# Seven-product MLP layers after retention: lo parts moved to VectorE, weights converted in units of 1024 columns, PSUM and row sums laid out anew, one activation instead of two operations

## The chip, the core and the metric

The kernel runs on one core of a Trainium2 chip. TensorE (PE) multiplies matrices out of SBUF into PSUM, VectorE (DVE), ScalarE (ACT) and GpSimd (POOL) compute on tiles of 128 partitions, and SyncE (SP) issues the DMAs. Every engine works through its own queue in order and waits on semaphores for the others. The metric is the device time of one launch in microseconds (us); three runs of the kernel before took 704.94 to 706.64 us, median 705.31.

## The reference

```python
# retention: per head a decaying state, step by step over 768 positions
for t in range(S):
    state = gamma * state + einsum('bhd,bhe->bhde', k[:, :, t], v[:, :, t])
    y[:, :, t] = scale * einsum('bhd,bhde->bhe', q[:, :, t], state)
x = y.transpose(0, 2, 1, 3).reshape(1536, 512)
x = (x @ w_a) * (x @ w_b) @ w_out                  # layer 1: 512 -> 1536 -> 512
h = x @ w_in                                       # layer 2: 512 -> 2048 -> 512
out = (h * (1.0 / (1.0 + exp(-1.702 * h)))) @ w_out2
```

There are 2 sequences of 768 tokens, 8 heads of 64. q, k and v are float32; the five weight matrices arrive as 64-bit floats.

## The kernel before, in words

**Retention.** 12 blocks (2 sequences of 6) of 128 tokens. For block n TensorE computes the scores of block n+1 (`att_scores`, L199), the state's increment (`att_kv`, L227) and the output (`att_av`: from the scores, L245, and from the state, L256). VectorE masks the scores (L208), ScalarE copies the state out of PSUM (L237). POOL scales q and v by decays (`att_q` L174, `att_v` L182) for later blocks. `att_x` copies the output and, on every second block, forms the sums that the next stage wants.

**Exact products from float32r.** TensorE multiplies in the rounded format float32r. So each operand is split: hi is the rounded value (a ScalarE copy with a cast), lo = value - hi (`lo_part`, L65, a TENSOR_TENSOR on POOL or VectorE), and each product is three matmuls: hi x hi, hi x lo, lo x hi.

**Seven products.** The up products (x times `w_a`, `w_b` or `w_in`) are done on 2 x 2 blocks with seven block products instead of eight. The row operands are a11 and a12 (tile `a1`), a22, and four sums (`s12`, `s34`); the weight operands are b11, b21, b22 and four sums made by VectorE (L68, tile `tt`). A `Job` is one pair of 128-column chunks of one up matrix: 12 jobs in layer 1 (six pairs for each of `w_a` and `w_b`), 8 in layer 2. Its seven steps of 12 matmuls (L494, 384 columns) accumulate in three PSUM sets of two banks (x, y, w), with copies and adds between them: ScalarE copies x to y after step 1, keeps `u2` and `u4` after steps 6 and 5, VectorE adds and multiplies into the result `g` (L71, L74), and some multiplies `g<-g,u` go to POOL. In layer 2 `result` runs Sigmoid on ScalarE (L516) and then the multiply. `up_order` interleaves the steps of neighbouring jobs. PSUM is used as two pools of two sets each (`ps_a`, `ps_b`).

**Down products.** `down` multiplies chunks of `g` (split into `ghl`) by the down weights, in blocks of four chunks (FB), for four quarters q of the output: per chunk 3 x 3 matmuls of 512 columns (L673). Two quarters share three PSUM sets. After each block `flush` copies (first block, ScalarE L688) or adds (VectorE L71) PSUM into row sums in SBUF. Six chunks stay in SBUF, the others are spilled to DRAM and loaded again. After layer 1's last block `y_part` makes layer 2's row operands out of the row sums.

**Weights.** A piece is 512 columns of 64-bit words (`wraw`). ScalarE takes the absolute value of the high word (L345) and shifts the low word (L346). VectorE clamps (L351), shifts (L352), sets the sign (L358) and adds the low bits (L364): `wt`. Then come the sums, hi (L377) and lo (L65, on POOL). `w_stream` is a generator; each call of `w_step`, one after each step of the up and down stages, emits the next bit of it. 68 pieces in all.

**What sets the order.** The tile scheduler is off (`tc.manual_schedule`): every engine's queue holds its instructions in the order in which the Python code emits them. So a queue's head that waits holds everything behind it, on VectorE, ScalarE and POOL alike.

Of the kernel before, what the change touches and what calls it, by code (L numbers as in the profile page):

```python
# [15 lines left out]
P = 128  # L16
# [24 lines left out]
def retention_moe_kernel(  # L41
# [25 lines left out]
    def sub(engine, o, a, b):  # L67
        engine.tensor_tensor(out=o, in0=a, in1=b, op=ALU.subtract)  # L68

    def add(engine, o, a, b):  # L70
        engine.tensor_tensor(out=o, in0=a, in1=b, op=ALU.add)  # L71
# [40 lines left out]
    vinv = attp.tile([P, SEQ, H, 1], F32, tag="vinv", name="vinv", bufs=1)  # L112
    gdec = attp.tile([P, SEQ, NP], F32, tag="gdec", name="gdec", bufs=1)
    qdec = attp.tile([P, SEQ, NP, P], F32, tag="qdec", name="qdec", bufs=1)
    zero = attp.tile([P, P], F32, tag="zero", name="zero", bufs=1)

    state = [attp.tile([P, NP, 2, D], F32, tag=f"state{i}", name=f"state{i}", bufs=1) for i in range(2)]
    qv_t, kk_t, q_t, v_t, a_t, x_t = {}, {}, {}, {}, {}, {}
# [52 lines left out]
    def att_q(n):  # L171
        if n < NBLK:
            t = attp.tile([P, NP, P], F32, tag="q", name="q", bufs=3)
            (nc.vector if n == 1 else nc.gpsimd).tensor_tensor(  # L174
                out=t, in0=qv_t[n][:, 0, :].rearrange("p (a t) -> p a t", t=P), in1=qdec[:, n % SEQ], op=ALU.mult
            )
            q_t[n] = t

    def att_v(n):
        if n < NBLK:  # L180
            t = attp.tile([P, H, D], F32, tag="v", name="v", bufs=3)
            nc.gpsimd.tensor_tensor(  # L182
                out=t,
                in0=qv_t[n][:, 1, :].rearrange("p (h d) -> p h d", d=D),
                in1=vdec[:, n % SEQ].to_broadcast([P, H, D]),
                op=ALU.mult,
            )
            v_t[n] = t

    def att_scores(n):  # L190
# [3 lines left out]
        ps = ps_a.tile([P, 2, G], F32, tag="set", name="ps_sc")  # L194
# [21 lines left out]
    def att_kv(n):  # L216
# [3 lines left out]
        if c == 0:  # L220
            kv_t[0] = ps_att.tile([P, NP, D], F32, tag="kv", name="ps_kv")
        ps = kv_t[0]
# [16 lines left out]
    def att_av(n):  # L239
        c = n % SEQ  # L240
        ps = ps_att.tile([P, NP, P], F32, tag="av", name="ps_av", bufs=2)
# [626 lines left out]
```

## Time and profile before

| | us |
|---|---|
| profiled execution, its span | 708.58, 706.8 |
| median of three runs | 705.31 |
| TensorE busy, VectorE, ScalarE, POOL | 608.6, 472.1, 307.4, 330.4 |
| retention (0 to 74 us of the span) | 74 |
| up 1 (74 to 269), 1008 matmuls | 195 |
| down 1 (269 to 384), 432 matmuls | 115 |
| up 2 (384 to 541), 672 matmuls | 157 |
| down 2 (541 to 703), 576 matmuls | 162 |
| tail | 3.8 |

The stages follow one another on TensorE; their bounds are where its matmuls change from one line to the next. A matmul's record lasts longer than the distance to the next one, since matmuls are pipelined, so the pace is read from counts over a stretch. The granted clock of TensorE has two levels in this trace, 1.00 (2.4 GHz) and 0.50 (1.2 GHz). What a stage loses is the time between what its matmuls need at full clock and its length.

### The profile page before, as it was taken

The numbers are of one execution on the slowest core, as the hardware profiler recorded it, in microseconds if no ns is written. First come the engines' busy times: TensorE is split into PE (matmuls) and PEld (weight loads), VectorE is DVE, ScalarE is ACT, GpSimd is POOL, SyncE is SP. The second block draws the span as 40 slices with busy tenths as digits, with TensorE's granted clock in tenths as the row PEclk, the third lists the DMA queues.
The fourth block names the chain that finished last, engine by engine and source line by source line (L and its number), as shares of the span: only waits on it lengthen the run. The fifth ranks groups of instructions, "written<-read, shape, count | busy, mean of one in ns | idle before, by whom it ended". The sixth has DMA issues, their size and how long they took to land. (4 is left out here: it accounts for less than half of the span.)

```text
span 706.8 us, 8931 instructions
## 1 busy us (share of the span) xinstructions
PE 608.6 (86%) x3446; PEld 547.9 (78%) x3446; DVE 472.1 (67%) x541; ACT 307.4 (43%) x479; POOL 330.4 (47%) x279
## 2 busy tenths in 40 slices
PE   9777898999999957899997499999885497899997
PEld 8676798999999956777776489988885375677775
DVE  3658789999898999752448566777889919222222
ACT  4536554654464564361213465566685425111000
POOL 6565246474463546545313335555556708243100
PEclk9978899999999987899999599999998799799999
DMA  9662224442522324513000114445332531212022
GB/s 314 197 213 102 59 90 149 119 154 86 179 60 62 119 89 158 184 46 120 30 1 0 59 51 151 157 182 189 107 117 56 196 108 45 89 48 87 1 77 102
DMA packets 21707, 76.94 MB, mean 109 GB/s; under 512 B 2336, under 2 KB 2464, under 8 KB 21664
## 3 DMA queue, kind: packets, MB, share of 16 engines
q1 hardware_dynamic: 21088, 75.77, 31.8%
q10 hardware_dynamic: 576, 0.59, 0.3%
q8 instruction: 27, 0.44, 0.2%
q14 instruction: 16, 0.13, 0.1%
HBM read 60.62 MB, written 15.73 MB: 108 GB/s over the span
## 5 line engine op out<-in xcount | busy, mean ns | idle before, releaser
L673 PE MATMUL ps<-w,ghl 128*128 128x512 f32 x576 | 138.4, 402 | 23.2 <-DVE sum L71 13.4
L673 PEld LDWEIGHTS ps<-w,ghl 128*128 128x128 f32 x576 | 111.3, 194 | 50.1 <-DVE sum L71 15.9
L65 POOL TENSOR_TENSOR w<-wt,w 128x512 fp32r<-128x512 f32 (+1 forms) x68 | 86.4, 1271 | 99.8 <-ACT w L377 82.1
L673 PE MATMUL ps<-ghl,w 128*128 128x512 f32 x432 | 102.1, 397 | 12.2 <-ACT sum L688 7.1
L71 DVE TENSOR_TENSOR sum<-ps,sum 128x512 f32<-128x512 f32 (+1 forms) x41 | 36.7, 933 | 113.5 <-PE ps L673 105.5
L673 PEld LDWEIGHTS ps<-ghl,w 128*128 128x128 f32 x432 | 82.4, 192 | 31.8 <-ACT sum L688 7.9
L65 POOL TENSOR_TENSOR ghl<-g,ghl 128x1536 fp32r<-128x1536 f32 x22 | 79.3, 3622 | 45.4 <-ACT ghl L579 45.1
L494 PE MATMUL ps<-a1h,w 128*128 128x384 f32 x320 | 79.1, 351 | 15.4 <-ACT ps L531 6.9
L65 POOL TENSOR_TENSOR w<-tt,w 128x512 fp32r<-128x512 f32 x40 | 58.0, 1450 | 69.9 <-ACT w L377 44.2
L494 PE MATMUL ps<-s34h,w 128*128 128x384 f32 x320 | 77.0, 348 | 10.6 <-ACT u L540 6.2
L364 DVE CUSTOM_DVE_ANT_0 wt<-wraw,wt 128x1024 uint16<-128x1024 uint16 x68 | 78.6, 1156 | 6.4 <-DVE wt L358 0.5
L74 POOL TENSOR_TENSOR g<-g,u 128x768 f32<-128x768 f32 x28 | 56.3, 2010 | 56.4 <-ACT g L516 35.6
L377 ACT CAST w<-wt 128x512 fp32r<-128x512 f32 (+1 forms) x68 | 37.7, 555 | 91.1 <-DVE wt L364 62.0
L494 PE MATMUL ps<-s12h,w 128*128 128x384 f32 x320 | 74.9, 336 | 1.8 <-ACT u L537 1.4
L358 DVE SCALAR_TENSOR_TENSOR wt<-wraw,wt 128x512 int32<-128x512 int32 x68 | 73.7, 1084 | 1.4
L494 PEld LDWEIGHTS ps<-a1h,w 128*128 128x128 f32 x320 | 60.4, 199 | 17.6 <-ACT ps L531 7.4
L351 DVE TENSOR_SCALAR wt<-wt 128x512 f32<-128x512 f32 x68 | 55.1, 811 | 24.9 <-ACT wt L345 24.9
L352 DVE TENSOR_SCALAR wt<-wt 128x512 int32<-128x512 int32 x68 | 68.3, 1005 | 2.3
L494 PEld LDWEIGHTS ps<-s34h,w 128*128 128x128 f32 x320 | 58.1, 194 | 15.0 <-ACT u L540 8.9
L579 ACT CAST ghl<-g 128x1536 fp32r<-128x1536 f32 x28 | 40.5, 1473 | 60.7 <-PE ps L673 35.7
L494 PE MATMUL ps<-a,w 128*128 128x384 f32 x240 | 48.2, 352 | 15.7 <-DVE u L71 15.7
L494 PEld LDWEIGHTS ps<-s12h,w 128*128 128x128 f32 x320 | 56.9, 188 | 3.1 <-ACT u L537 2.1
(77 smaller groups left out, 866.8 us busy)
## 6 DMA issues: line engine op xcount, KB each, us to landing
wraw<-in_w_dram SPq DMA_DIRECT2D x68, 512.0 KB, 3.7
spilled<-g SPq DMA_DIRECT2D x16, 768.0 KB, 4.8
g<-spilled SPq DMA_DIRECT2D x16, 768.0 KB, 4.9
qv<-in_att_dram SPq DMA_DIRECT2D x11, 512.0 KB, 6.1
kk<-in_att_dram SPq DMA_DIRECT2D x9, 512.0 KB, 6.8
out_dram<-sum SPq DMA_DIRECT2D x3, 512.0 KB, 2.8
out_dram<-sum SPq DMA_DIRECT2D x6, 256.0 KB, 2.4
kk<-in_att_dram SPq DMA_DIRECT2D x3, 256.0 KB, 5.9
```

Source lines behind the costliest of these rows:

```text
L65: engine.tensor_tensor(out=lo, in0=src, in1=hi.bitcast(F32), op=ALU.subtract)
L71: engine.tensor_tensor(out=o, in0=a, in1=b, op=ALU.add)
L74: engine.tensor_tensor(out=o, in0=a, in1=b, op=ALU.mult)
L351: nc.vector.tensor_scalar(out=t, in0=t, scalar1=F64_LOW, scalar2=F64_HIGH, op0=ALU.max, op1=ALU.min)
L352: nc.vector.tensor_scalar(out=ti, in0=ti, scalar1=3, scalar2=0x3FFFFFFF, op0=ALU.logical_shift_left, op1=ALU.bitwise_and)
L358: nc.vector.scalar_tensor_tensor(out=ti, in0=wraw[i][:, :, 1], scalar=-0x40000000, in1=ti, op0=ALU.bitwise_and, op1=ALU.bitwise_or)
L364: nc.vector.tensor_tensor(out=ti, in0=ti, in1=wraw.pop(i)[:, :, 0], op=ALU.add)
L377: nc.scalar.copy(hi, src)
L494: nc.tensor.matmul(ps[:, b, 0:Q], w_operand(self.key, i, wp)[:, kc * P:(kc + 1) * P], r.operand(i, xp)[:, kc, b * Q:(b + 1) * Q], start=(s ...
L579: nc.scalar.copy(g[:, 0], t)
L673: nc.tensor.matmul(banks[n], l, r, start=(f == block[0] and i == 0), stop=(f == block[-1] and i == 2), skip_group_check=True,)
```

## The change

Names are kept where they can be; line numbers move.

- **Lo parts.** `split` emits the hi copy on ScalarE and notes the lo part; `finish` emits noted lo parts on VectorE one step later. `POOL_LO` is empty, so no weight lo part goes to POOL, and `ghl` and the row operands' lo parts go to VectorE too. POOL keeps q, v and the 12 multiplies `g<-g,u` of layer 1's second matrix.
- **Units.** 34 units of 1024 columns take the place of 68 pieces of 512: a job's four weight blocks in one unit, or two chunks of down weights. Each of the conversion steps is one instruction of 1024 columns (the last reads 2048 half words). The operands lie in `wd` (768 columns: b12.. as loaded) and `wt` (1024: the sums, or two chunks).
- **Retention.** q and v are scaled in halves of 256 columns. Sums and lo parts read and write the output in PSUM (three sets instead of two) and are emitted one or two blocks later; some lo parts of `s34` and a22 wait in the list `later` until the up stage. The first unit is converted in blocks 5 to 12.
- **PSUM.** `ps_x` (two sets of two banks) serves scores, x, w and the down stages' first two groups; `ps_y` (two sets of two banks) the up stages and `ps_d` (four single banks) the down stages. Each quarter has its own sets. In `products` all six matmuls of one half b run before those of the other. The first job of layer 1 works in halves.
- **Row sums between the layers.** Layer 1's last block does the first 1024 columns of all four quarters, then the last 512 of quarters 0, 2, 1, 3. `y_first` splits the first halves on the way; `y_second` computes the sums in place, and their splits are taken from `later` in layer 2's first steps.
- **Layer 2.** Gelu_apprx_sigmoid on ScalarE writes `g` at once; the multiply is gone.

```diff
-    rawp = ctx.enter_context(tc.tile_pool(name="rawp", bufs=3))
-    wa = ctx.enter_context(tc.tile_pool(name="wa", bufs=WA))
-    ps_a = ctx.enter_context(tc.tile_pool(name="ps_a", bufs=2, space=PSUM))
+    rawp = ctx.enter_context(tc.tile_pool(name="rawp", bufs=2))
+    wd = ctx.enter_context(tc.tile_pool(name="wd", bufs=2))
+    up_u = ctx.enter_context(tc.tile_pool(name="up_u", bufs=5))
+    ps_x = ctx.enter_context(tc.tile_pool(name="ps_x", bufs=2, space=PSUM))
...
+            for k in (slice(0, NP),) if n == 1 else (slice(0, 2), slice(2, NP)):
+                mul(nc.vector if n == 1 else nc.gpsimd, t[:, k], q[:, k], qdec[:, n % SEQ, k])
...
+    def split(dst, src, keys=()):
+        hi, lo = dst
+        nc.scalar.copy(hi, src)
+        pend.append((keys, lambda: lo_part(nc.vector, lo, src, hi)))
+    def finish(key=None):
+        for it in [it for it in pend if key is None or key in it[0]]:
+            pend.remove(it)
+            it[1]()
...
-        t = rawp.tile([P, DM, 2], I32, tag="wraw", name="wraw", bufs=3)
+        t = rawp.tile([P, W, 2], I32, tag="wraw", name="wraw", bufs=2)
...
+    def w_lo(kind, key, src):
+        whl[kind, key] = t = w_half.pop((kind, key))
+        n = src.shape[-1]
+        lo_part(nc.gpsimd if key in POOL_LO.get(kind, ()) else nc.vector, t[:, 1, 0:n], src, t[:, 0, 0:n])
...
+    POOL_LO = {}
...
-                for wp, xp in ((0, 0), (0, 1), (1, 0)):
-                    for b in range(2):
+            for b in range(2):
+                for kc in range(2):
+                    for wp, xp in ((0, 0), (0, 1), (1, 0)):
...
             if self.ph == 2:
-                nc.scalar.activation(out=g, in_=src, func=ACTF.Sigmoid, scale=1.702)
-            mul(nc.vector if u is None else nc.gpsimd, g, g, src)
+                nc.scalar.activation(out=g, in_=src, func=ACTF.Gelu_apprx_sigmoid)
+            else:
+                mul(nc.vector if u is None else nc.gpsimd, g, g, src)
...
+        shape = dict(y=2, d=4)[name]
...
+        return pool.tile([P, G] if which == "d" else [P, 2, G], F32, tag="set", name="ps")
...
+            if last and ph == 1:
+                for q in range(4):
+                    a = new_set("x")
+                    for f in block:
+                        product(q, f, (0, 1), [a[:, 0], a[:, 1]])
+                        tick(fb)
+                    flush(q, [(a.rearrange("p c t -> p (c t)"), 0, 2 * G)])
+                    y_first(q, sums)
+                for q in (0, 2, 1, 3):
...
+                    if q >= 2:
+                        y_second(q - 2, sums)
```

POOL's queue in the middle of retention, before (numbers tell tiles of one name apart):

```order
L182 TENSOR_TENSOR v_432<-qv_203,vdec_76 128x512
L65 TENSOR_TENSOR s34l_363<-s_467,s34h_362 128x4x128
L174 TENSOR_TENSOR q_489<-qv_312,qdec_79 128x512
L182 TENSOR_TENSOR v_491<-qv_240,vdec_76 128x512
L174 TENSOR_TENSOR q_539<-qv_384,qdec_79 128x512
L182 TENSOR_TENSOR v_541<-qv_312,vdec_76 128x512
L65 TENSOR_TENSOR s34l_363<-s_566,s34h_362 128x4x128
```

and in the changed kernel:

```order
L75 TENSOR_TENSOR q_429<-qv_243,qdec_81 128x256 x2
L75 TENSOR_TENSOR v_432<-qv_204,vdec_79 128x256 x2
L75 TENSOR_TENSOR q_485<-qv_316,qdec_81 128x256 x2
L75 TENSOR_TENSOR v_488<-qv_243,vdec_79 128x256 x2
L75 TENSOR_TENSOR q_541<-qv_374,qdec_81 128x256 x2
```

The lo part between v and the next q is no longer in this queue; q and v come in halves (x2).

VectorE's queue in the changed kernel where up 1 begins, from the first job's last operand (`wt_913`) to the second job's first (`wd_1007`); before, the lo parts of `s34` and of the weights among them were in POOL's queue:

```order
L66 TENSOR_TENSOR wt_913<-tt_820,wt_913 128x1024
L66 TENSOR_TENSOR s12l_427<-x_870,s12h_426 128x4x128
L66 TENSOR_TENSOR s34l_450<-x_526,s34h_449 128x4x128
L66 TENSOR_TENSOR a22_451<-x_526,a22_451 128x2x128
...
L66 TENSOR_TENSOR s34l_450<-x_845,s34h_449 128x4x128
L409 TENSOR_SCALAR wt_825<-wt_825 128x1024
L410 TENSOR_SCALAR wt_825<-wt_825 128x1024
L416 SCALAR_TENSOR_TENSOR wt_825<-wraw_626,wt_825 128x1024
...
L422 ISA wt_825<-wraw_626,wt_825 128x2048
L69 TENSOR_TENSOR tt_1009<-wt_825 128x256 x2
...
L66 TENSOR_TENSOR wd_1007<-wt_825,wd_1007 128x768
```

Left out are two more pairs of `s34l` and a22, one add into `g` and the other two sums. The lo parts of four earlier blocks now stand ahead of the second job's weights.

VectorE's queue where layer 1 ends, before:

```order
L71 TENSOR_TENSOR sum_2839<-ps_3187,sum_2839 128x1024
L71 TENSOR_TENSOR sum_2839<-ps_3146,sum_2839 128x512
L65 TENSOR_TENSOR a1l_3092<-sum_2839,a1h_3091 128x768
L71 TENSOR_TENSOR s_3267<-sum_2770,sum_2839 128x768
L68 TENSOR_TENSOR s_3267<-s_3267,sum_2770 128x768
L65 TENSOR_TENSOR s12l_3221<-s_3267,s12h_3220 128x2x768
```

and in the changed kernel:

```order
L72 TENSOR_TENSOR sum_2585<-ps_2987,sum_2585 128x512
L66 TENSOR_TENSOR a22_2966<-sum_2585,a22_2966 128x768
L69 TENSOR_TENSOR sum_2490<-sum_2490 128x768
L72 TENSOR_TENSOR sum_2490<-sum_2490,sum_2585 128x768
L69 TENSOR_TENSOR sum_2585<-sum_2585,sum_2490 128x768
L69 TENSOR_TENSOR sum_2585<-sum_2585 128x768
L66 TENSOR_TENSOR s12l_3032<-sum_2531,s12h_3031 128x768
L66 TENSOR_TENSOR wt_3001<-tt_2883,wt_3001 128x1024
L66 TENSOR_TENSOR s12l_3032<-sum_2585,s12h_3031 128x768
```

Before, the lo part of a1 (which layer 2's first step reads) stood behind the last quarter's row sum; now it is split earlier, and what follows the last row sum are the in-place sums and the parts of `s12`.

## Rows read from the trace of the kernel before

**Rows 1.** Busy time by stage: window, five engines, clock, DMA share, GB/s.

```profile
0.00:74.00 74.00, 57.75 (x758) 52.30 (x758) 45.59 (x62) 36.13 (x80) 42.36 (x117) 0.86 0.59 197
74.00:269.00 195.00, 181.62 (x1007) 178.79 (x1008) 175.61 (x212) 105.03 (x172) 99.28 (x67) 0.96 0.33 106
269.00:384.00 115.00, 102.83 (x437) 83.12 (x436) 66.10 (x66) 39.79 (x53) 49.18 (x23) 0.96 0.24 83
384.00:541.00 157.00, 127.50 (x670) 122.19 (x669) 117.66 (x146) 90.83 (x136) 82.11 (x51) 0.91 0.33 115
541.00:703.00 162.00, 138.76 (x580) 111.54 (x578) 66.43 (x57) 35.60 (x42) 57.47 (x22) 0.94 0.25 86
```

**Rows 2.** Two windows of matmuls alone (PE, PEld, clock), and the last matmuls.

```profile
160.00:240.00 80.00, 80.00 (x464) 80.00 (x463) 1.00 0.30 95
...
684.00:696.00 12.00, 12.00 (x55) 9.93 (x54) 1.00 0.20 74
...
697.32 5.78 PE L673 MATMUL ps<-w,ghl 128*128 128x512 f32 x24 [0.78 <-DVE sum L71]
```

**Rows 3.** TensorE's waits: releaser, total us, times, longest.

```profile
PE ps L673 <- DVE sum L71: 18.5, 10, 7.7
PE ps L673 <- ACT sum L688: 17.0, 4, 8.9
PE ps L494 <- DVE u L71: 16.2, 3, 8.3
```

**Rows 4.** Timeline, end of up 1 and in down 2: start, duration, [idle before].

```profile
258.00 4.24 POOL L65 TENSOR_TENSOR ghl<-g,ghl 128x1536 fp32r<-128x1536 f32 x1 [0.65 <-ACT ghl L579]
258.89 3.64 DVE L351 TENSOR_SCALAR wt<-wt 128x512 f32<-128x512 f32 x1
...
264.57 0.95 DVE L71 TENSOR_TENSOR u<-ps,u 128x768 f32<-128x768 f32 x1
...
265.57 4.21 PE L494 MATMUL ps<-a,w 128*128 128x384 f32 x12 [8.33 <-DVE u L71]
...
592.73 7.25 POOL L65 TENSOR_TENSOR ghl<-g,ghl 128x1536 fp32r<-128x1536 f32 x2 [1.03 <-ACT ghl L579]
596.75 3.52 DVE L352 TENSOR_SCALAR wt<-wt 128x512 int32<-128x512 int32 x1
603.61 2.93 PE L673 MATMUL ps<-w,ghl 128*128 128x512 f32 x6 [7.66 <-DVE sum L71]
```

**Rows 5.** Single operations: count, ns shortest/median/longest, first and last start.

```profile
L351 DVE TENSOR_SCALAR wt<-wt x68: 409/419/3721, 58.6 to 593.0; 128x512 f32<-128x512 f32 x68
L352 DVE TENSOR_SCALAR wt<-wt x68: 426/430/3551, 59.1 to 596.7; 128x512 int32<-128x512 int32 x68
L358 DVE SCALAR_TENSOR_TENSOR wt<-wraw,wt x68: 675/725/3848, 63.0 to 600.3; 128x512 int32<-128x512 int32 x68
L364 DVE CUSTOM_DVE_ANT_0 wt<-wraw,wt x68: 691/693/3784, 63.7 to 601.1; 128x1024 uint16<-128x1024 uint16 x68
L65 POOL TENSOR_TENSOR w<-wt,w x68: 738/1296/2701, 69.4 to 626.7; 128x512 fp32r<-128x512 f32 x48, 128x256 fp32r<-128x256 f32 x20
L65 DVE TENSOR_TENSOR ghl<-g,ghl x6: 1746/1752/2856, 254.4 to 535.2; 128x1536 fp32r<-128x1536 f32 x6
L516 ACT ACTIVATE g<-u x16: 842/848/858, 420.3 to 543.5; 128x768 f32<-128x768 f32 x16
```

**Rows 6.** The page's costliest groups, one of VectorE: busy us, mean ns.

```profile
L364 DVE CUSTOM_DVE_ANT_0 wt<-wraw,wt 128x1024 uint16<-128x1024 uint16 x68 | 78.6, 1156 | 6.4 <-DVE wt L358 0.5
```

**Rows 7.** Timeline of retention: two blocks' first matmuls, and a late q.

```profile
14.23 1.16 PE L199 MATMUL ps_sc<-q,kk 64*128 64x128 f32 x16 [0.23 <-POOL q L174]
...
17.69 1.16 PE L199 MATMUL ps_sc<-q,kk 64*128 64x128 f32 x16
...
33.23 1.26 POOL L65 TENSOR_TENSOR s34l<-s,s34h 128x512 fp32r<-128x512 f32 x1 [4.50 <-ACT s34h L291]
...
35.96 2.08 PE L199 MATMUL ps_sc<-q,kk 64*128 64x128 f32 x16 [2.35 <-POOL q L174]
```

More of the change, by code (lines that the diff above doesn't have):

```diff
@@ L65, in lo_part, with sub, add @@
         engine.tensor_tensor(out=lo, in0=src, in1=hi.bitcast(F32), op=ALU.subtract)
[L67 to L71, printed above, removed]
+    def sub(o, a, b):
+        nc.vector.tensor_tensor(out=o, in0=a, in1=b, op=ALU.subtract)
+    def add(o, a, b):
+        nc.vector.tensor_tensor(out=o, in0=a, in1=b, op=ALU.add)
     def mul(engine, o, a, b):
@@ new lines, in product, with used @@
+            def product(q, f, ns, banks):
+                w_need(("t", d_unit(f)))
+                finish(f)
+                while f not in ghl:
+                    before = split_at[ph]
+                    g_next(ph, fb * FB + FB)
+                    assert split_at[ph] > before, f
+                    finish(f)
+                down_products(ph, q, f, ns, banks, block)
+            def used(f):
+                room["big"] += 1
+                ghl.pop(f)
+                if f in block[1::2]:
+                    w_free("t", d_unit(f))
@@ new lines, in flush @@
+            def flush(q, spans):
+                if fb == 0:
+                    sums[q] = row_tile("sum")
+                t = sums[q].rearrange("p h b t -> p (h b t)")
+                for src, a, b in spans:
+                    if fb == 0:
+                        nc.scalar.copy(t[:, a:b], src)
+                        continue
+                    add(t[:, a:b], src, t[:, a:b])
+                    if ph == 2 and last:
+                        half, seq = divmod(q, 2)
+                        rows = out.rearrange("(b j h p) d -> p b h j d", b=B, h=2, p=P)[:, seq, half]
+                        n = slice(a // G, b // G)
+                        nc.sync.dma_start(out=rows[:, n, :], in_=t[:, a:b].rearrange("p (j d) -> p j d", d=DM))
@@ new lines, in down @@
+            for q in range(4):
+                if last and q == 3:
+                    a = new_set("x")
+                    banks = [a[:, 0], a[:, 1], new_set("d")]
+                    for n in range(NG):
+                        for f in block:
+                            product(q, f, (n,), banks)
+                        flush(q, [(banks[n], n * G, (n + 1) * G)])
+                    continue
+                a, d = new_set("x"), new_set("d")
+                for f in block:
+                    product(q, f, range(NG), [a[:, 0], a[:, 1], d])
+                    if q == 3:
+                        used(f)
+                    tick(fb)
+                flush(q, [(a.rearrange("p c t -> p (c t)"), 0, 2 * G), (d, 2 * G, NT)])
@@ new lines, in y_half, with y_first, y_second @@
+    def y_half(t, half):
+        return t.rearrange("p h b t -> p h (b t)")[:, half]
+    def y_first(q, sums):
+        r = rows_of[2]
+        split([r.a1(i)[:, q] for i in range(2)], y_half(sums[q], 0), (("row", 1),))
+    def y_second(kc, sums):
+        r = rows_of[2]
+        a11, a21 = (y_half(sums[kc], h) for h in range(2))
+        a12, a22 = (y_half(sums[2 + kc], h) for h in range(2))
+        split([r.a22(i)[:, kc] for i in range(2)], a22, (("row", 4),))
+        finish()
+        sub(a11, a11, a21)
+        add(a21, a21, a22)
+        sub(a22, a22, a11)
+        sub(a12, a12, a22)
+        for two, op, src in ((0, 1, a22), (0, 0, a21), (1, 0, a11), (1, 1, a12)):
+            later.append(lambda two=two, op=op, src=src: split(
+                [r.s(two, i)[:, op, kc] for i in range(2)], src, (("row", (5, 7)[two]),)
+            ))
+        if kc == 1:
+            later[:] = [later[k] for k in (0, 4, 1, 5, 2, 6, 3, 7)]
```

565 lines of the change are left out of this document (293 added, 272 removed).

## The prediction

> **What bounds the kernel now.** I read the busy times by stage first, then TensorE's pace in a stretch without waits, then the list of its waits, then the stretches around the longest ones, and last the durations of single operations.
>
> The stage windows [rows 1] show five stages of 74, 195, 115, 157 and 162 us: retention, up 1, down 1, up 2, down 2, and 3.8 us of tail. TensorE is busy in most of each and its mean clock is 0.86, 0.96, 0.96, 0.91 and 0.94, so each stage loses time twice: by gaps, and by the half clock (1.2 GHz) behind some gaps. What it would take without either follows from its pace: between 160 and 240 us, at clock 1.00, 464 matmuls of 384 columns are counted in 80 us, less two that began before it 0.173 us each; 55 of 512 columns in 12 us, less two, 0.227 us [rows 2]. The four products stages hold 1008, 432, 672 and 576 matmuls, so at that pace they need 1008 x 0.173 = 174.4, 432 x 0.227 = 98.1, 672 x 0.173 = 116.3 and 576 x 0.227 = 130.8 us. Beside 195, 115, 157 and 162 they lose 20.6, 16.9, 40.7 and 31.2 us: 109 us in all, retention not counted.
>
> Who takes it: TensorE waits for VectorE's row sums (18.5 us in 10 waits), ScalarE's copies of row sums (17.0 in 4) and VectorE's adds in the up stages (16.2 in 3) [rows 3]. Behind the long ones is one thing. At the end of up 1 POOL begins a lo part of 1536 columns at 258.0 that takes 4.24 us; a TENSOR_SCALAR of VectorE begins at 258.9 and takes 3.64 us, ending when POOL's does; the add behind it comes at 264.6, and TensorE has stood for 8.33 us. Its next twelve matmuls take 4.21 us where 12 x 0.173 is 2.1, the half clock [rows 4]. In down 2 two lo parts of POOL, 7.25 us from 592.7, hold a TENSOR_SCALAR until 600.3, and TensorE stands 7.66 us for the row sum behind it [rows 4]. Alone a TENSOR_SCALAR takes 0.41 us. The four conversion steps take 409, 426, 675 and 691 ns at their shortest and up to 3.55 to 3.85 us [rows 5]; the last is 1156 ns in the mean over 68 [rows 6].
>
> **The change, part by part.**
> *VectorE without POOL's lo parts.* The weight lo parts, `ghl`'s and those of the row operands leave POOL, which keeps q and v in retention and 12 multiplies in up 1. So the 3 to 4 us blocks go. VectorE gets the lo parts at its own price: 768 columns take 0.95 us [rows 4], 1536 take 1746 ns [rows 5], which is 154 ns + 1.036 per column: 0.42, 0.68 and 1.21 us at 256, 512 and 1024. No row has a TENSOR_SCALAR of 1024 columns; its 512 at 409 ns is what 256 of the two-input kind cost by this law, so it is between 0.68 (two columns at a time) and 1.21; I take 0.68, the law that its own row obeys. A converted unit of 1024 columns is then 0.68 + 0.68 + 1.21 + 1.23 (the last by doubling 691 less 154) = 3.8 us; 34 units make 129 us. Two old pieces alone are 4.4 us. A job in an up stage adds four sums (1.7), lo parts of 768 and 1024 (2.2) and, on the mean, three (up 1) or two (up 2) operations of 768 columns at 0.95 [rows 4]: 10.5 and 9.6 us, against TensorE's 84 x 0.173 = 14.5 us. VectorE stays below TensorE at the 1.21 end too (11.6).
> The row shows a VectorE operation and a POOL one ending together [rows 4]. The Trainium skill, "SBUF — State Buffer", Who interferes with whom, calls this an exclusive lock: the later of the two stands for the whole of the other, if VectorE's has two SBUF inputs or a two-port mode. It speaks against the change where POOL still works; what the trace allows there is priced under retention.
>
> *Retention, 74 us.* Before, POOL's queue holds the lo part of `s34` between its q's; POOL stands 4.50 us for ScalarE's hi part, q comes after, TensorE waits 2.35 [rows 7]. After, q and v alone are on POOL, in halves. A block without a wait takes 17.69 - 14.23 = 3.46 us [rows 7]; eleven blocks from 14.2 end at 52. POOL's four halves at 738 ns (its shortest 256-column operation [rows 5]) are 3.0 us, just below. VectorE has 6.6 us per two blocks by the law above, and in blocks 6 to 10 the first weight unit, 3.8 + 1.7 + 2.2 = 7.7: 5 x 3.3 + 7.7 = 24.2 beside 17.3, so 6.9 us more than TensorE's pace, less what it can run behind, say 5. Some 12 of its operations there have two SBUF inputs or are TENSOR_SCALARs; each can wait for a POOL half, 0 to 0.74 us: 0 to 9, I take 3. So up 1 begins at 60 (52 to 68): -14.
>
> *Up 1, 195 us.* 174.4 and the waits. In the order, VectorE has eight small lo parts, one unit's conversion and its lo part before the second job's first operand: from `wt_913` to `wd_1007` 1.2 + 5 x 0.68 + 3 x 0.42 + 3.8 + 0.95 + 1.7 + 0.95 = 13.3 us. `wt_913` starts after ScalarE's cast, that is after the first product (2.1) and 1.0: so 16.4 us in. TensorE has six products before it, 12.5 us: 3.9 us of wait, and about 2.5 us of half clock after it, by what the 8.33 us wait cost (2.1) [rows 4]. 2 us for scattered waits. The end's 8.33 us goes: of the lo parts between the last adds each is 1.75, and one `ghl` part and one weight part (3.0 us) pass under two products (4.2). 183: -12.
>
> *Down 1, 115 us.* The row-sum adds no longer wait behind locked conversions. The accumulators are two sets of two banks and four single banks, so a set is wanted again 16 us after its sum, where an add takes 1.2 + 0.7. VectorE's work there, by the order's counts and the law, is 14 (eight `ghl`) + 25 (five units and their lo parts) + 15 (eight pairs of row-sum adds) + 19 (the next layer's sums and lo parts) = 73 us of 99. 98.1 + 1 = 99: -16.
>
> *Up 2, 157 us.* The first four products need only the first halves, split before the last sums. From TensorE's last matmul: two adds 1.4 (behind about 1 us of the previous sums), hi 0.85, lo 0.95, four subtracts 3.8, then `s12l` parts with a weight lo part between: the second is done at about 11 us, TensorE arrives after 8.3. I take 3 us there, 3 at `s34` three products on (ScalarE has twelve casts, copies and conversions there, 10 us at the 0.85 of the nearest row [rows 5], in 10 us), 3 us of half clock, and 3.5 us scattered. The multiplies after the activation go: 16 on VectorE, 16 on POOL. Gelu_apprx_sigmoid has no row; Sigmoid's is 848 ns [rows 5]. From 0.85 to twice that: 32 x 0.85 = 27 us more on ScalarE, 3.4 a job on about 10 of 14.5, at worst some 2 us of wait per job, 16 in all. I take 0.85. 116.3 + 12.5 = 129: -28.
> The Trainium skill, "ScalarE: Activation LUTs", Step-by-step, says that the engine takes one element a cycle whatever the function; by it the upper end is nothing. No run here shows it yet.
>
> *Down 2, 162 us.* As down 1: 130.8 + 1.5 = 132: -30. The tail stays.
>
> Sum: -14 - 12 - 16 - 28 - 30 = -100. The profiled execution took 708.6 us (span 706.8 and 1.8 around it), the median of the runs is 705.3, a factor 0.995. 608.6 x 0.995 = 606 us.
>
> **The rivals.**
> *Nothing new waits.* Retention at TensorE's pace (52) and every stage at its pace: 52 + 174.4 + 98.1 + 116.3 + 130.8 + 3.8 + 1.8 = 577, with the usual few waits 577 to 588. For it: the mid-stage stretches of before already run without gaps [rows 2]. Against: the two chains counted out above.
> *VectorE is late all the same.* If its conversions keep the factor of the last step, 1156 / 691 = 1.67 [rows 5, 6], a unit is 6.3 us and an up 1 job 13.0 of 14.5: on the mean enough, but its bursts reach TensorE as before. Then up 1 keeps most of its loss (+12) and up 2 half (+15): 633. For it: all lo parts are now on one in-order queue. Against: POOL has 12 operations left after retention, where it had 68 weight lo parts from `wt` alone [rows 5].
> *Slower.* Products now send six matmuls in a row into one bank, where two banks took turns. If each then had to end before the next began, a matmul would cost what its own first one after a wait costs, at most its record of some 0.33 us for 0.173: 1680 x 0.16 = 269 us, 875 us. It decides from 0.06 us per matmul on. Against it: the last 24 matmuls of before go twelve and twelve into one bank each, and take 5.78 us [rows 2], 0.24 us each with the pipe's fill, as with three banks in turn.
>
> **How the numbers follow.** Forecast 78 in 100, with its own range 590 to 628 (retention 52 to 68, the waits of 24 us after it between 10 and 35). Nothing waits 8, VectorE late 12, slower 2. A range that leaves out no more than 2 in 10 takes in most of the late case and a part of the early one: 588 to 640. Of faster by over 0.3% (2 us, about what a measurement tells from no change) I give 0.97, no change 0.01, as the far end of the late case, slower 0.02.
>
> **What would show it.** Right: VectorE's 1024-column TENSOR_SCALARs near 0.68 us and none over 2 in the down stages; no wait over 2 us within a stage; one of 3 to 5 us on the second job of up 1 and two at the start of up 2; up 1 beginning near 60. Wrong: matmuls of 384 columns at more than 0.18 us; TensorE waiting for VectorE's `u` or row sums by several us; an activation of 1.7 us; retention above 70.

## The result and the profile after

The changed kernel takes 609.66 us (median of 4 runs, 608.51 to 611.0), the kernel before 705.97 (704.94 to 707.18) beside it: ratio 0.8636, 95% interval 0.8607 to 0.8665. The forecast was 606. The profiled execution of the changed kernel, the longest of its four, took 611.0 us, 609.2 of them span, so its stages are read against that.

The stage windows of the changed kernel answer to [rows 1]; columns as there.

```profile
0.00:59.00 59.00, 51.42 (x762) 46.58 (x763) 38.16 (x57) 34.25 (x77) 36.79 (x133) 0.94 0.77 265
59.00:246.00 187.00, 178.52 (x1010) 175.66 (x1008) 150.33 (x177) 95.01 (x112) 26.45 (x11) 0.99 0.29 99
246.00:347.00 101.00, 98.28 (x433) 80.96 (x433) 70.42 (x73) 39.87 (x40) 2.72 (x1) 1.00 0.31 110
347.00:474.00 127.00, 120.36 (x674) 117.98 (x673) 89.87 (x108) 86.26 (x101) 0.00 (x0) 0.99 0.35 129
474.00:606.00 132.00, 130.67 (x575) 107.51 (x574) 71.96 (x67) 40.55 (x37) 0.00 (x0) 1.00 0.32 114
```

The granted clock is close to 1.00 in every stage but the first, POOL is idle from up 1's end on, and 74, 195, 115, 157 and 162 us have become 59, 187, 101, 127 and 132.

TensorE's pace, in a stretch of up 2 and one of down 2 without waits (columns: stretch, busy time and matmuls of TensorE, clock, DMA share, GB/s; for [rows 2]):

```profile
380.00:460.00 80.00, 80.00 (x463) 1.00 0.48 179
```
```profile
490.00:590.00 100.00, 100.00 (x443) 1.00 0.27 95
```

Less the two that began before, 80 / 461 = 0.174 us and 100 / 441 = 0.227 us: as before. Six matmuls in a row into one bank cost nothing here.

TensorE's longest sums of waits (for [rows 3]; waited for: us in total, times, longest):

```profile
PE ps_sc L198 <- DMA kk<-in_att_dram: 4.8, 3, 3.8
PE ps L605 <- DVE wd L66: 3.0, 3, 1.5
PE ps L605 <- ACT wd L434: 2.9, 2, 1.6
PE ps L605 <- ACT u L656: 2.1, 2, 1.4
PE ps L835 <- DVE g L75: 2.1, 1, 2.1
...
PE ps L835 <- DVE sum L72: 1.4, 2, 0.8
```

The row sums fell from 18.5 + 17.0 us to 1.4, VectorE's adds in up stages are gone from the head of the list, and a load in the retention leads it.

VectorE's conversion steps on 1024 columns (for [rows 5, 6]; busy us, mean ns | idle before; L409 by ns shortest/median/longest), and the new activation (in the same way):

```profile
L422 DVE CUSTOM_DVE_ANT_0 wt<-wraw,wt 128x2048 uint16<-128x2048 uint16 x34 | 43.3, 1273 | 1.4
L416 DVE SCALAR_TENSOR_TENSOR wt<-wraw,wt 128x1024 int32<-128x1024 int32 x34 | 41.5, 1221 | 0.6
L410 DVE TENSOR_SCALAR wt<-wt 128x1024 int32<-128x1024 int32 x34 | 26.6, 783 | 1.2
```
```profile
L409 DVE TENSOR_SCALAR wt<-wt x34: 679/685/2343, 40.6 to 553.8; 128x1024 f32<-128x1024 f32 x34
```
```profile
L631 ACT ACTIVATE g<-ps x16: 789/814/818, 356.1 to 472.6; 128x768 f32<-128x768 f32 x16
L631 ACT ACTIVATE g<-u x16: 844/847/852, 375.4 to 477.5; 128x768 f32<-128x768 f32 x16
```

### The profile page after: what moved, and what is told of

It reads as the page before. It is cut to its first block, busy times and chain, and to the rows that moved or that the text cites. A ratio compares the mean times of both kernels' runs of the same rounds, so it can differ in the third digit from the quotient of the medians.

```text
span 609.2 us, 8443 instructions
## 1 busy us (share of the span) xinstructions
PE 579.2 (95%) x3448; PEld 528.7 (87%) x3448; DVE 420.9 (69%) x478; ACT 295.9 (49%) x366; POOL 66.0 (11%) x145
## 4 chain that ended last, share of the span: by engine, by line
PE 75%; DVE 14%; ACT 4%; DMA 4%; issue 3%; POOL 0%; ACTq 0%; DVEq 0%
PE ps L605 36%; PE ps L835 34%; DMA kk<-in_att_dram 3%; PE ps_sc L198 2%; DVE tt L69 2%; DVE wt L422 1%; DVE sum L72 1%; PE ps_av L244 1%; DVE wt L416 1%; DVE s34l L66 1%; DVE sum L69 1%; PE ps_kv L226 1%; ACT wraw L404 1%; ACT wt L403 1%; DMA causal<-in_cmask_dram 1%
## 5 line engine op out<-in xcount | busy, mean ns | idle before, releaser
L835 PE MATMUL ps<-wt,ghl 128*128 128x512 f32 x576 | 131.1, 389 | 0.8 <-DVE sum L72 0.8
L835 PEld LDWEIGHTS ps<-wt,ghl 128*128 128x128 f32 x576 | 108.0, 188 | 23.6 <-DVE sum L72 1.2
L835 PE MATMUL ps<-ghl,wt 128*128 128x512 f32 x432 | 98.7, 390 | 2.7 <-DVE g L75 2.1
L835 PEld LDWEIGHTS ps<-ghl,wt 128*128 128x128 f32 x432 | 80.9, 188 | 20.2 <-DVE g L75 2.6
L605 PE MATMUL ps<-a1h,wd 128*128 128x384 f32 x320 | 89.2, 341 | 7.8 <-DVE wd L66 3.0
L605 PE MATMUL ps<-s12h,wt 128*128 128x384 f32 x320 | 87.4, 335 | 1.0 <-ACT u L654 1.0
L605 PEld LDWEIGHTS ps<-a1h,wd 128*128 128x128 f32 x320 | 59.3, 192 | 10.0 <-DVE wd L66 4.0
L605 PEld LDWEIGHTS ps<-s12h,wt 128*128 128x128 f32 x320 | 58.3, 188 | 1.6 <-ACT u L654 1.4
L605 PE MATMUL ps<-s12l,wt 128*128 128x384 f32 x160 | 53.7, 336 | 1.5 <-DVE s12l L66 1.5
L605 PE MATMUL ps<-a1l,wd 128*128 128x384 f32 x160 | 54.2, 339 | 0.0
```

The costliest lines, as they stand in the source:

```text
L605: nc.tensor.matmul(ps[b][:, 0] if len(ps) > 1 else ps[0][:, b], w_operand(self.key, i, wp)[:, kc * P:(kc + 1) * P], r.operand(i, xp)[:, kc ...
L835: nc.tensor.matmul(banks[n], l, r, start=(f == block[0] and i == 0), stop=(f == block[-1] and i == 2), skip_group_check=True,)
```

## The experiments

Twelve kernels, each with 4 timed runs beside the kernel before. The table gives the stage lengths in us in their profiled executions, from each stage's first matmul to the next one's.

| kernel | median us | ratio to before [95%] | retention | up 1 | down 1 | up 2 | down 2 |
|---|---|---|---|---|---|---|---|
| before | 705.97 | 1 | 74.1 | 195.5 | 114.1 | 157.7 | 161.7 |
| changed | 609.66 | 0.8636 [0.8607, 0.8665] | 58.6 | 186.9 | 101.3 | 126.8 | 131.9 |
| e1 weight lo on POOL | 622.95 | 0.8838 [0.8807, 0.8869] | 56.0 | 195.3 | 104.3 | 129.3 | 131.9 |
| e2 ghl lo on POOL | 614.18 | 0.8705 [0.8669, 0.8742] | 56.2 | 188.4 | 104.7 | 126.8 | 133.9 |
| e3 Sigmoid, multiply | 621.56 | 0.8794 [0.8761, 0.8827] | 54.4 | 188.4 | 102.9 | 136.9 | 134.2 |
| e7 all three | 648.30 | 0.9184 [0.9147, 0.9221] | 56.4 | 195.9 | 103.6 | 149.4 | 135.9 |
| e11 shared third banks | 670.05 | 0.9476 [0.9448, 0.9503] | 57.1 | 188.4 | 130.2 | 125.2 | 163.7 |
| e4 banks in turn | 606.99 | 0.8591 [0.8556, 0.8626] | 55.6 | 187.4 | 101.2 | 124.8 | 131.9 |
| e5 unit loaded early | 605.23 | 0.8583 [0.8560, 0.8606] | 53.5 | 186.9 | 101.3 | 126.7 | 131.9 |
| e10 retention lo on POOL | 604.08 | 0.8555 [0.8530, 0.8579] | 57.0 | 180.7 | 102.8 | 126.8 | 131.9 |
| e12 e4 + e5 + e10 | 601.01 | 0.8514 [0.8491, 0.8537] | 55.5 | 180.6 | 101.3 | 124.8 | 131.9 |
| e6 before, lo on VectorE | 718.38 | 1.0189 [1.0166, 1.0212] | 71.6 | 185.4 | 129.3 | 151.8 | 174.7 |
| e8 before, own banks | 663.60 | 0.9396 [0.9377, 0.9414] | 73.0 | 193.9 | 98.7 | 159.4 | 133.0 |
| e9 e6 + e8 | 667.21 | 0.9446 [0.9429, 0.9464] | 70.5 | 186.5 | 106.7 | 155.5 | 142.3 |

Where a kernel leaves the retention as changed, that stage took 54.4 to 58.6 us: it varies by 4 us from run to run, so a retention is compared with that spread.

### Undoing a part of the changed kernel

**e1**, the weight lo parts on POOL again.

```diff
-    POOL_LO = {}
+    POOL_LO = {k: [u[1:] for u in units] for k in "dt"}
```

> The changed kernel with the lo parts of all weight tiles (34 of 1024 columns, 20 of 768) emitted on POOL again; everything else as changed. VectorE has 34 x 1.22 + 20 x 0.95 = 60 us less to do. Theory (VectorE and POOL hold each other up, and that made the row sums and adds late): slower than the changed kernel in spite of the smaller load, 625 to 655 us; VectorE's TENSOR_SCALARs of 1024 columns, 0.68 us alone, are stretched beside POOL's lo parts, many to over 1.5 us, and operations that read PSUM are not. Rival (what counted was only how much VectorE has to do, or the units of 1024 columns): 600 to 610 us, and no operation stretched.

13 us slower than the changed kernel although VectorE has less to do, a little under the range expected; 8.4 us of it in up 1, nearly as much as up 1 had won. The first conversion step of e1 (compare L409 above):

```profile
L409 DVE TENSOR_SCALAR wt<-wt x34: 680/1272/2367, 38.5 to 565.3; 128x1024 f32<-128x1024 f32 x34
```

Its median is 1272 instead of 685 ns, and 14 of the 34 take more than 1.5 us; the adds that read PSUM (`u<-ps,u`, `sum<-ps,sum`) keep their length, as expected. So lo parts on POOL do hold VectorE up. On the way to TensorE this goes through ScalarE, late in up 1 of e1:

```profile
197.25 2.03 POOL L66 TENSOR_TENSOR wd<-wt,wd 128x768 fp32r<-128x768 f32 x1
...
197.60 1.95 DVE L72 TENSOR_TENSOR tt<-tt,wt 128x256 f32<-128x256 f32 x1
...
200.04 1.05 ACT L434 CAST wt<-tt 128x1024 fp32r<-128x1024 f32 x1 [4.09 <-DVE tt L69]
...
203.88 0.44 PE L605 MATMUL ps<-s34h,wd 128*128 128x384 f32 x1 [2.58 <-ACT u L656]
```

A weight sum of 0.42 us takes 1.95 beside POOL's lo part, ScalarE's cast waits 4.09 us for the sums, and the copy of `u`, which TensorE wants, comes behind the cast. TensorE's waits in up 1 grow from 8.5 to 14.2 us: by 4.5 for ScalarE's copies, and by 1.1 for the lo parts of `wd`, which are now POOL's.

**e2**, the lo parts of `ghl` on POOL again (`split(..., nc.gpsimd)` in `g_split`).

> The changed kernel with the 28 lo parts of ghl (1536 columns, 1.75 us on VectorE) emitted on POOL again, at about 3.6 to 4.3 us each there. Theory: the stretches that held VectorE for 3.5 us before come back; TensorE waits for row sums in the down stages and at the end of up 1: down 1 from 101 to about 106, down 2 from 132 to about 140, up 1 some 3 us more, 620 to 630 us in all. Rival (with a set of its own for each quarter a late row sum no longer reaches TensorE): within 3 us of 609.7.

4.5 us slower: 3.4 in down 1, 2.0 in down 2, 1.5 in up 1. The direction was the theory's, the size nearer to the rival's: 28 parts of some 3.5 us on POOL, yet only four waits for row sums, 6.0 us in all where the changed kernel has 1.4, and no wait stands at the end of up 1.

**e3**, Sigmoid and a multiply in layer 2.

```diff
-                nc.scalar.activation(out=g, in_=src, func=ACTF.Gelu_apprx_sigmoid)
-            else:
-                mul(nc.vector if u is None else nc.gpsimd, g, g, src)
+                nc.scalar.activation(out=g, in_=src, func=ACTF.Sigmoid, scale=1.702)
+            mul(nc.vector if u is None else nc.gpsimd, g, g, src)
```

> The changed kernel with Sigmoid and a multiply in layer 2 in place of the one activation: 32 activations of the same length as now, and 16 multiplies of 768 columns on VectorE (0.95 us) and 16 on POOL (about 1.9 us). Theory: VectorE's load in up 2 goes from 90 to 106 of 127 us, and the POOL multiplies hold some of its conversions for up to 1.9 us; up 2 gets 3 to 9 us longer, 613 to 619 us. Rival (VectorE has room enough and TensorE never waits for it there): within 2 us of 609.7.

12 us slower, up 2 10.1 us longer, a little above the range. Beside VectorE's load there is a cause that no theory had. The timeline of e3 at a product of up 2 (start, us, engine, line, operation, [idle before, what ended it]):

```profile
428.51 0.79 ACT L631 ACTIVATE g<-ps 128x768 f32<-128x768 f32 x1
...
429.39 0.95 DVE L75 TENSOR_TENSOR g<-g,ps 128x768 f32<-128x768 f32 x1 [3.79 <-issue]
...
430.40 0.45 PE L605 MATMUL ps<-s34h,wt 128*128 128x384 f32 x1 [0.82 <-DVE g L75]
```

The multiply reads the product in PSUM after the activation has, so the set comes free about 1 us later; TensorE stands for it three times for 2.7 us in all. The rest of the 10.1 us was not taken apart.

**e7**, e1, e2 and e3 together, and the row operands' lo parts that go through `split` on POOL too.

> The changed kernel with three parts undone together: the lo parts of weights, of ghl and of the row operands that go through split on POOL, and Sigmoid with a multiply in layer 2. Theory (a held-up VectorE hurts more the more POOL has to do, because the lateness of one reaches the other): more than the sum of the single prices, 650 to 680 us, with waits of several us for row sums in the down stages. Rival (the prices add up: 609.7 + 13 + 4.5 + 12): 636 to 643 us.

38.6 us slower, where e1, e2 and e3 add up to 29.7. Between the two forecasts: 22.6 us of it lie in up 2, with 5.5 us of waits for POOL's `s34l` and 3.4 for its `s12l`, the parts that only e7 moves. The down stages stay within 4 us of the changed kernel, against the theory: POOL's lo parts are back and TensorE still waits only 4.2 us for row sums.

**e11**, the third banks of two successive quarters in one tile, as before.

```diff
...
+        if which == "d":
+            if not half_d:
+                t = more["ps_d"].tile([P, 2, G], F32, tag="set", name="ps")
+                half_d.extend([t[:, 1], t[:, 0]])
+            return half_d.pop()
```

> The changed kernel with the third banks of two successive quarters in one tile of two banks, as before; everything else as changed. Theory: TensorE stands at the third matmul of every second quarter for the copy or add of the row sum, at least 1.2 us each, 6 times in down 1 and 8 times in down 2, and for several us where VectorE has a lo part or a conversion in hand: down 1 from 101 to 108 to 115, down 2 from 132 to 142 to 150, the whole 627 to 645 us. Rival (with VectorE free of POOL the sums come in time and the shared set costs nothing): 608 to 612 us.

60 us slower, all in the down stages (28.9 and 31.8), with POOL idle there. Far above the range: no other single edit cost or won as much. TensorE's waits in e11:

```profile
PE ps L843 <- DVE sum L72: 30.6, 11, 6.4
PE ps L843 <- ACT sum L787: 15.1, 4, 7.1
```

One of them, in down 2:

```profile
546.31 1.76 DVE L66 TENSOR_TENSOR ghl<-g,ghl 128x1536 fp32r<-128x1536 f32 x1 [1.82 <-ACT ghl L272]
547.99 1.22 DVE L422 CUSTOM_DVE_ANT_0 wt<-wraw,wt 128x2048 uint16<-128x2048 uint16 x1
549.12 1.75 DVE L66 TENSOR_TENSOR ghl<-g,ghl 128x1536 fp32r<-128x1536 f32 x1
...
553.93 1.76 DVE L66 TENSOR_TENSOR ghl<-g,ghl 128x1536 fp32r<-128x1536 f32 x1 [3.06 <-ACT ghl L272]
555.61 1.22 DVE L66 TENSOR_TENSOR wt<-wt 128x1024 fp32r<-128x1024 f32 x1
556.74 1.81 DVE L72 TENSOR_TENSOR sum<-ps,sum 128x1024 f32<-128x1024 f32 x2
...
558.61 3.78 PE L843 MATMUL ps<-wt,ghl 128*128 128x512 f32 x8 [6.41 <-DVE sum L72]
```

VectorE stands 3.06 us for a cast of `ghl`, does two lo parts, and only then the row sum for which TensorE has stopped. In the changed kernel VectorE has the same queue, but there TensorE may go on for a quarter meanwhile.

**e4**, the halves of a product in turn, as before (`b` the innermost loop of `products`).

> The changed kernel with the matmuls of each product in the order of before: the two halves b, which lie in two PSUM banks, in turn, instead of six matmuls in a row into one bank. Theory: a matmul into the bank of the one before it costs nothing more, so no change: within 2 us of 609.7, and 0.173 us per matmul in both. Rival (a bank wanted twice in a row costs something): the pace falls below 0.173 us and the whole gets shorter by 1680 times the difference.

The pace is the same (464 matmuls where 463 stood, in the same 80 us). The whole is 2.7 us below the changed kernel, a little outside the theory's 2 us but with overlapping intervals: unclear by itself. In its trace up 2 is 2.0 us shorter, and the waits for VectorE's lo parts (`wd`, `s12l`, `s34l`) come to 3.5 us instead of 6.2. With `b` innermost the first matmul on a lo operand is the third of twelve, or the fifth where the weight's lo part is meant, instead of the second and the third, which would explain shorter waits; that was not tested apart.

### Doing a part alone on the kernel before

**e6**, all of POOL's lo parts on VectorE, one step later.

```diff
         nc.scalar.copy(hi, src)
-        lo_part(nc.gpsimd, lo, src, hi)
+        pend.append((key, lambda: lo_part(nc.vector, lo, src, hi)))
...
```

> The kernel before with one part of the change alone: all lo parts that POOL had (weights, ghl, row operands) on VectorE, those of weights and ghl one step later than their hi part. Pieces of 512 columns, PSUM, order and Sigmoid with its multiplies as before. Theory (the holding up of VectorE by POOL is the main cause of the 96 us): 640 to 665 us, with the waits for row sums in the down stages mostly gone (down 2 from 162 to under 140). Rival A (the prices of the undone parts add up, 13 us for the weights and 4.5 for ghl): 680 to 692 us. Rival B (the layout of PSUM, units and order give the gain, and VectorE has no room for it with pieces of 512): 695 to 715 us.

All forecasts fall: 12.6 us (1.9%) slower than before, beyond rival B's 695 to 715 too. Up 1 wins 10.1 us and up 2 5.9; the down stages lose 15.2 and 13.0. The three waits of [rows 3], 18.5, 17.0 and 16.2 us before, are now:

```profile
PE ps L683 <- DVE sum L71: 33.1, 10, 11.7
PE ps L683 <- ACT sum L698: 26.3, 4, 12.9
...
PE ps L503 <- DVE u L71: 2.7, 3, 1.7
```

So without POOL's lo parts the adds of the up stages come in time, while the waits for row sums grow. The longest wait but one, in down 2, shows VectorE's queue without POOL's lo parts:

```profile
594.48 3.43 DVE L65 TENSOR_TENSOR ghl<-g,ghl 128x1536 fp32r<-128x1536 f32 x2 [1.79 <-ACT ghl L588]
...
600.59 1.47 ACT L588 CAST ghl<-g 128x1536 fp32r<-128x1536 f32 x1 [4.76 <-DMA g<-spilled]
...
602.09 1.76 DVE L65 TENSOR_TENSOR ghl<-g,ghl 128x1536 fp32r<-128x1536 f32 x1 [2.86 <-ACT ghl L588]
...
606.49 1.81 DVE L71 TENSOR_TENSOR sum<-ps,sum 128x1024 f32<-128x1024 f32 x2
608.36 4.21 PE L683 MATMUL ps<-w,ghl 128*128 128x512 f32 x9 [11.71 <-DVE sum L71]
```

ScalarE stands 4.76 us for a spilled chunk's load, VectorE 2.86 us for ScalarE, and the row sum is behind both.

**e8**, the third bank of each quarter in a set of its own; POOL keeps its lo parts.

```diff
-                    for s in (2 * at, 1) if at == 0 else (2,):
+                    for s in (2 * at, 1):
...
-                    banks = [sets[2 * at][:, 0, :], sets[2 * at][:, 1, :], sets[1][:, at, :]]
+                    banks = [sets[2 * at][:, 0, :], sets[2 * at][:, 1, :], sets[1][:, 0, :]]
```

> The kernel before with one part of the layout of PSUM alone: in the down stages each quarter's third bank lies in a set of its own, where two quarters shared a set of two banks (in the trace TensorE does 36 + 2 matmuls and then stands at the third of the second quarter until the first quarter's row-sum add is done). POOL keeps its lo parts. Theory (the shared set makes every late row sum reach TensorE at once; with its own set a sum may be a quarter late, 8 to 16 us): the waits for row sums, 18.5 + 17.0 us in 14, mostly go, down 1 from 114 to about 103, down 2 from 162 to about 138: 665 to 680 us. Rival (the sums are late because POOL holds VectorE, and a later wait takes their place): 695 to 706 us.

42 us faster than before, 1.4 us below the range: these two lines bring down 1 to 98.7 and down 2 to 133.0, where the changed kernel has 101.3 and 131.9. Its windows of the down stages:

```profile
267.00:366.00 99.00, 99.00 (x436) 81.93 (x435) 67.98 (x63) 38.10 (x51) 49.62 (x23) 0.99 0.27 95
...
525.00:658.00 133.00, 131.45 (x578) 107.72 (x576) 66.22 (x56) 35.38 (x41) 57.40 (x22) 1.00 0.29 103
```

and POOL, which works on in them for 49.62 and 57.40 us, still holds VectorE:

```profile
L351 DVE TENSOR_SCALAR wt<-wt x68: 410/420/3736, 57.7 to 564.6; 128x512 f32<-128x512 f32 x68
```

So the holding up cost the down stages nothing by itself; what cost them was that a late row sum reached TensorE at once.

**e9**, e6 and e8 together.

> The kernel before with two parts of the change: all lo parts of POOL on VectorE (which alone made it 1.9% slower) and the third bank of each quarter in a set of its own. Theory: with a quarter of slack the bursts on VectorE's queue (lo parts that stand for ScalarE's casts) no longer reach TensorE in the down stages: down 1 about 101 to 104, down 2 133 to 137, the whole 645 to 660 us, that is less than with either part alone. Rival (lo parts on VectorE harm wherever they stand, so the two prices add up): 12 us more than with the banks alone, 677 to 692 us.

667.21: neither range. Lo parts on VectorE cost 12.6 us with shared banks and still 3.6 with own banks; up 1 wins 7.4 there, the down stages lose 8.0 and 9.3 against e8. So the move to VectorE pays in the changed kernel (e1, e2), not in the order of work of before. Which part of the new order makes the difference was not taken apart; one that the code shows is that `tick` splits one `ghl` a step, where `g_next` split all that had room.

### Going further

**e5**, the first unit's load after block 0: `W_LOADS, LATER = (0, 6), (9,11)`.

> The changed kernel with the load of the first weight unit (1 MB) issued after block 0 of the retention instead of block 2, ahead of the qv and kk loads of the later blocks, in a stretch where the transfers pause for want of free buffers. Theory: the wait of 2.2 to 3.8 us for kk near 32 us comes from the unit's transfer, which shares the 400 GB/s of that stretch with the loads behind it; the wait goes, and with it the half clock after it: retention 51 to 54 us instead of 54.4 to 58.6, the whole 604 to 607 us. Rival (the loads of q, k and v alone fill the stretch): the wait stays, 609 us.

605.23, within the theory's range, with the other stages within 0.1 us and the retention at 53.5. The waits for `kk` go from 4.8 (longest 3.8) to 2.1 (longest 1.1), and the `kk` issued at 24.35 us lands after 6.35 us, where the same load, issued at 24.46 in the changed kernel, took 11.16. So the load behind the unit's transfer does come sooner. How much that is worth is less sure: 53.5 is only 0.9 us below the shortest retention of the spread, and the intervals of the two ratios all but touch (0.8606 and 0.8607).

**e10**, the retention's lo parts of `s34` and a22 on POOL at once, not noted for later.

```diff
-            later.append(lambda: [lo_part(nc.vector, lo, src, hi) for (hi, lo), src in parts])
+            for (hi, lo), src in parts:
+                lo_part(nc.gpsimd, lo, src, hi)
...
```

> The changed kernel with the lo parts of s34 and a22 in the retention on POOL, in its queue between the q and v of the blocks, as s34's were before, and not noted for later. Theory (POOL stands at them for ScalarE's hi part and q and v come late): retention 60 to 66 us instead of 54.4 to 58.6, TensorE waiting for POOL's q in every second block; but VectorE has eight small lo parts (4.4 us) less at the start of up 1, whose waits shrink by 2 to 4 us: in all 611 to 618 us. Rival (POOL has room in its queue, and only the start of up 1 changes): 604 to 608 us.

The rival's number, 604.08. The retention stays at 57.0, within its spread: POOL stands 8.9 us for ScalarE's `s34h`, and TensorE waits for POOL's v for 1.0 us in all. Up 1 wins 6.2 us: the list `later` is shorter, so the second job's unit is converted sooner, and TensorE's waits in up 1 fall from 8.5 to 4.2 us.

**e12**, e4, e5 and e10 together.

> The changed kernel with three edits together: the first weight unit loaded after block 0, the lo parts of s34 and a22 in the retention on POOL, and the two halves of a product in turn. Theory: the gains over the changed kernel (4.4, 5.6 and 2.7 us) come from other waits (kk in the retention, the second job's operands in up 1, operands in up 1 and 2) and mostly add up: 597 to 601 us. Rival (loading early and the lo parts on POOL gain from the same waits, or POOL is late with q and v once kk comes in time): 602 to 605 us.

601.01 us, between the edges of the two ranges; ratio 0.8514 against 0.8636, with intervals apart: 1.4% faster than the changed kernel, 8.7 us of the 12.7 that the three gains add up to. Up 1 and up 2 are those of e10 and e4; the retention, 55.5, is within its spread and does not reach e5's 53.5.

## Why the prediction was right, and where its reasons were not

**Sizes.** Forecast 60, 183, 99, 129 and 132 us by stage, measured 58.6, 186.9, 101.3, 126.8 and 131.9: no term is off by more than 3.9 us, and the misses partly cancel. (The retention of 58.6 is the longest of the 54.4 to 58.6 seen.) That sum rests on one decision that holds: take TensorE's pace times its matmuls as the length of each stage and count what waits remain. The reasons given for the waits that go are a different matter.

**Down 1 and down 2** (-12.8 and -29.8 in the traces, 44% of the gain): the step that failed in its reason. The prediction put these waits down to conversions held by POOL [rows 4] and named the accumulators in passing, as a reserve. That the number came out is luck as far as this reason goes: the same change brought both, and the move of the lo parts alone (e6) made the two stages 28 us longer. e8 and e11 show that the shared third bank decides, in both directions: -44.1 us in the two stages by it alone with POOL's lo parts in place, +60.7 by its return with POOL idle. The rows stood in the trace of before, in down 2:

```profile
639.82 0.84 PE L673 MATMUL ps<-w,ghl 128*128 128x512 f32 x3
640.02 1.82 DVE L71 TENSOR_TENSOR sum<-ps,sum 128x1024 f32<-128x1024 f32 x2 [6.28 <-PE ps L673]
641.90 16.63 PE L673 MATMUL ps<-w,ghl 128*128 128x512 f32 x72 [1.24 <-DVE sum L71]
649.73 1.82 DVE L71 TENSOR_TENSOR sum<-ps,sum 128x1024 f32<-128x1024 f32 x2 [7.88 <-PE ps L673]
657.89 1.82 DVE L71 TENSOR_TENSOR sum<-ps,sum 128x1024 f32<-128x1024 f32 x2 [6.34 <-PE ps L673]
659.77 0.50 PE L673 MATMUL ps<-w,ghl 128*128 128x512 f32 x1 [1.24 <-DVE sum L71]
```

A quarter is 36 matmuls. After every second row sum, and only there, TensorE stops for 1.24 us although the sum begins at once; 72 matmuls lie between two such stops, and each comes at the third matmul of a quarter, the first into the tile that the quarter before still holds. Of the ten waits for row sums in [rows 3], 18.5 us, one is the 7.66 us of [rows 4]; eight, 10.0 us together, are of this kind, 1.24 or 1.35 us each. A wait that recurs with nothing late is a dependency without slack, and then whatever makes VectorE or ScalarE late (POOL in before, a load and a cast in e6, lo parts in e11) is paid in full. The two quarters' banks in that tile are different ones; whether a finer dependency would do without the wait was not tried.

**Up 1** (-8.6): the reason holds for the kernel before. e6 takes POOL's lo parts away, and the 8.33 us at the end of the stage become 1.73. In the changed order of work that wait does not come back when `ghl`'s lo parts return to POOL (e2, e7), so that order is without it either way; e1's 8.4 us are other waits, earlier in the stage. By the Trainium skill's "SBUF — State Buffer", Who interferes with whom, the later one waits for the whole of the other; the longest first steps of e1 and e8 agree within some 0.2 us: 2367 and 3736 ns instead of 685 and 420, each begun within 0.1 us after a lo part of POOL, of 1847 and 3546 ns.

The waits of the changed kernel were forecast as one of 3.9 us at the second job. The chain behind it, counted as 13.3 us, took 12.4, and the wait is 1.30 and 1.02. Not counted were 1.62 and 0.51 at the third job and 1.49 at the fourth, whose units come late in turn (probably since each job starts with what the last one left; not tested), and 1.82 at the first job's copy. That makes 8.5 us of waits in all for the 3.9 + 2 of the sum, the larger part of the miss of 3.9. e10 shows what the eight small lo parts in that chain cost: 6.2 us.

**Up 2** (-30.9): Gelu_apprx_sigmoid at 814 and 847 ns is Sigmoid's length (796 and 847 in e3), the lower end, as taken; by the Trainium skill's "ScalarE: Activation LUTs", Step-by-step, that was to be, and the trace agrees. The forecast counted the multiplies that go only as load; they also held PSUM sets (2.7 of e3's 10.1 us). e7 brings back 22.6 of the 30.9. The other 8.3 are not taken apart; e8, which has the old start of layer 2, stands there 6.5 us for a row sum and 7.8 for a copy. The new waits at the start, forecast at 3 + 3 and 3 of half clock, came to 1.5 for `s12l`, 1.7 for `s34l`, and one stretch of 3.4 us at half clock.

**Retention** (-15.5): the number was right (60, 58.6), the reason did not suffice. It named POOL's lo part of `s34` between the q's [rows 7]. TensorE did wait for POOL's q, 11.3 us in 5 waits; e6 takes the lo part off POOL and these waits fall to 0.9, but the stage keeps 71.6 us, because 14.8 us of waits for VectorE's mask and ScalarE's copies stand there instead. And e10 puts the lo part back on POOL at no loss. What e6 still has is the old order, in which a block's sums and casts are emitted at once:

```profile
22.49 1.26 DVE L68 TENSOR_TENSOR s<-x 128x256 f32<-128x256 f32 x1
...
23.78 0.62 ACT L291 CAST s34h<-s 128x512 fp32r<-128x512 f32 x1 [1.98 <-DVE s L68]
24.31 0.40 ACT L294 CAST a<-x 128x256 fp32r<-128x256 f32 x1
...
24.61 0.74 ACT L237 COPY state<-ps_kv 64x256 f32<-64x256 f32 x2
...
25.50 0.69 PE L227 MATMUL ps_kv<-v,kk 128*64 128x64 f32 x16 [3.64 <-ACT state L237]
```

The copy of the state, which TensorE wants, stands behind casts that wait for VectorE. That the later emission of sums and lo parts gives most of the gain is likely by these rows but not shown: it was not run alone, and neither were the third PSUM set and the halves of q and v. Not forecast at all were the wait of 3.79 us for `kk` (e5 shortens it) and one of 2.14 us at the start of down 1, for a multiply of VectorE: the sign "no wait over 2 us within a stage" failed there.

**VectorE's prices** held: 685 + 694 + 1224 + 1224 ns (medians), 3.83 us a unit for 3.8, and no single operation of 1.9 us or more after POOL's last multiply. **The rivals:** nothing new waits (577 to 588) failed on the waits counted; VectorE late all the same (633) did not come; the slower one fell with the unchanged pace, here and in e4.

## What to carry to other kernels

When a wait has an in-order queue behind it, ask first how much slack the waiting engine has: here a wait of constant length after every second block, with nothing late, was a shared buffer, and giving each user its own was worth more than speeding up what came late. Moving work to a free engine or off a contended one must be judged with the order of that engine's queue: lo parts on VectorE won some 18 us in one order of emission (e1 and e2 added up) and lost 13 in another (e6). A sum of stage lengths can be right for reasons that are wrong, so undo each part once.

## What was not expected of the hardware

- The 3 us that the prediction took for POOL's halves in the retention came to 1.0: three of VectorE's operations with all inputs in SBUF took 0.19, 0.35 and 0.45 us more than their shortest. Its operations that read PSUM were not held up by POOL. All 12 masks of the changed kernel took 1.210 to 1.225 us, 6 of them wholly beside POOL; one:

```profile
25.74 1.22 DVE L207 TENSOR_TENSOR a<-ps_sc,causal 128x1024 f32<-128x1024 f32 x1 [1.22 <-PE ps_sc L198]
...
25.94 1.18 POOL L75 TENSOR_TENSOR v<-qv,vdec 128x256 f32<-128x256 f32 x2
```

- A load of 512 KB that was issued behind others landed late as a whole: the `kk` for which TensorE waited was issued at 24.46 us, behind 1 MB of weights and a load of q and v, and landed 11.16 us later. The first two loads of the kernel, of 256 KB each, landed in 3.66 and 4.08 us.
